# A list schedule for GateLoop and a SwiGLU feed-forward block: new transfer times and a new table of stage dates

## The chip, the cores and the metric

The kernel runs on one core of a Trainium2 chip. The time is that of one execution on the device, in microseconds (us). TensorE is called PE here, VectorE DVE, ScalarE ACT, GpSimd POOL, and SyncE SP; PEld are the weight loads of PE. SP issues most of the transfers, ACT and POOL a few.

## The reference

Inputs are q, k, v and complex gates a_re, a_im of shape (batch 4, heads 8, sequence 768, head size 48), and three weights: 384 x 1536 twice (gate and value) and 1536 x 384 (out), with a scale of 384.

```python
scale = np.minimum(mag, 0.999) / (mag + 1e-06)       # mag = |a|
for t in range(S):
    new_re = ar * S_re - ai * S_im                   # ar, ai: the scaled gate
    new_im = ar * S_im + ai * S_re
    S_re, S_im = (new_re + kv, new_im)               # kv = outer(k[t], v[t])
    y[:, :, t] = np.einsum('bhd,bhde->bhe', q[:, :, t], S_re)
# y, heads joined, is x: 3072 tokens x 384
xn = x / np.sqrt(np.mean(x * x, axis=-1, keepdims=True) + 1e-06) * rms_g
g = xn @ w_gate
silu = g * (1.0 / (1.0 + np.exp(-g)))
out = silu * (xn @ w_val) @ w_out
```

## The kernel before

**Work.** The sequence is cut into 24 chunks of 128 tokens, six to a batch. The recurrence within a chunk is a causal attention: running products of the gates, as magnitude and angle, are multiplied into q and k, and then scores, a mask and a product with v give the chunk's output; a state of 96 x 384 carries the rest from chunk to chunk. The gates are worked out in 13 units: chunk 0, chunk 1, then pairs (2, 3), (4, 5) and so on. The feed-forward part works on groups of chunks: [0], [1], [2, 3], [4, 5], [6, 7], [8, 9], [10 to 13], [14 to 17], [18 to 21], [22, 23]. From the group [4, 5] on, the gate and value products share a bilinear scheme of 15 products in place of 18 (`joint`), and the out product one of 7 in place of 8 (`down`, per pair of chunks).

**Stages of a chunk**, by the names that the tables use. `load` brings a unit's a_re and a_im into `in`, `kq` its q and k into `kin`. `size`, `root`, `turn` work out magnitude and angle on ACT and DVE (squares, scans along the tokens, arctan, sines). `rot` multiplies them into q and k, in `rot` and `kin`, and then six transfers on SP (three from `rot` and three from `kin`; six from `rot` for the first four chunks) lay the result into `kq`, features on partitions. From chunk 4 on there is one `kq` buffer, written anew for each chunk when the last reader is done. `decay` sends the unit's end values the same way, in six small transfers. `attend` is the scores on PE (`bank<-kq`) and the masked copy into `am` on DVE; `y` the product with v (`am,ve`) and the old state (`kq,state`); `state` the transposed k and its product with v (`vn,kt`). `norm` squares the output on ACT, sums it on PE (`ones,sq`), takes the power -1/2 on POOL, spreads the result over partitions by two transfers on POOL's queue (`sq<-rs`, `row<-sq`, chunks 4 to 21) and multiplies it into `xT` on DVE. `head` and `feed` are the gate and value products (`xT,wg`, `xT,wv`, and sums of both), the silu on ACT and the product into `hT`. `down` and `plain` are the out product (`wo,hT`, `sums,extra`, `wo,extra`), and its result goes through `ot` to the output.

**Weights.** They come as twelve pieces of wide words on POOL's queue, two ahead (`raw`), and are narrowed on ACT and DVE (`w`). The same pieces are later looked at again for the range check (`look`), by transfers on SP. At the end a sum over all checks, `okc`, goes through PE into a flag `bad`, which every engine reads; if it is set, a second, general path computes the output. That path did not run here.

**What sets the order.** Nothing is issued while the program is written. Each instruction is recorded by `add` with a modelled duration, and reads and writes give its dependencies. `dates` works out a due date for each from its users' due dates, backwards, and then adds a shift for its stage from a table of numbers (`flow.shift`). `schedule` plays the engines through: whenever an engine is free, it takes the ready instruction with the least due date. The result is the order on each engine, which `issue` then emits; on the chip each engine keeps that order and waits where an operand is late. So a modelled duration or landing decides only where something stands, and so do the shifts.

A transfer's modelled landing is its issue, plus a lead, plus its load (served one after the other for all queues) and 0.05, plus a number `slow` of its own, plus `LAND`:

```python
served = t + o["load"] + 0.05
o["landed"] = served + o["slow"] + self.LAND
```

An instruction on PE that uses another tile shape than the one before it is charged `between`; an operand that comes from PE to another engine is charged `delay`. Matmuls put in as fillers (`bank<-rot`) keep PE busy at the start, where the plan shows idle time there.

Of the kernel before, what the change touches and what calls it, by code (L numbers as in the profile page):

```python
# [19 lines left out]
P = 128  # L20
C = 128
# [480 lines left out]
class Flow:  # L502
# [8 lines left out]
    LAND = 1.0  # L511
    LANES = 8
    turn = 0.0
# [238 lines left out]
def fast(tc, ctx, qT, kT, v, a_re, a_im, w_gate, w_val, w_out, rms_g, out, H, bad):  # L752
# [4 lines left out]
    D2 = 2 * D  # L757
# [3 lines left out]
    ND = DM // P  # L761
# [252 lines left out]
    def fetch(i, piece, raw, eng):  # L1014
# [12 lines left out]
        pace = dict(load=1.9 + 1.0e-3 * raw.shape[1], lead=1.2) if eng == "POOL" else dict(slow=2.5)  # L1027
# [63 lines left out]
    def way_of(u):  # L1091
        return u if u < 2 else 2 + u % 2

    def load_gates(u):
# [28 lines left out]
    def load_kq(u, t):  # L1123
        flow.stage = "kq", u
        for name, ap in (("q", qT), ("k", kT)):
            for i, n in enumerate(UNITS[u]):
                dma(t[name][:, i],
                    ap[n].rearrange("d (h t) -> (d h) t", t=C).rearrange("(j p) t -> p j t", p=P),
                    slow=0.5 if u < 2 else 1.5, behind=moved[HOLD] if u > 1 else rows_, group=("kq", u))
        return t  # L1130

    def send_decays(u):
# [8 lines left out]
        for r in range(2 * ND):  # L1141
            dma(decays[way_of(u)][r:D2:2 * ND], ends[:, r % ND, ns[0]:ns[0] + len(ns)], behind=moved[max(ns[0], 1)])

    def gates(u):
# [65 lines left out]
        for i, n_ in enumerate(ns):  # L1210
# [4 lines left out]
            moved[n_] = [dma(kq[r:D2:2 * ND], x, "ACT" if n_ == 0 and r % 3 == 1 else "SP", slow=0.3) for r, x in enumerate(rows[n_])]  # L1215
# [23 lines left out]
    def attend(n):  # L1239
# [5 lines left out]
        later = dict(slow=1.5 if n > 1 else 0.4, behind=moved[min(n - 1, HOLD)] if n else (), group=("v", n))  # L1245
# [408 lines left out]
    for in_, limit, op in ((ef, P_MIN, ALU.is_ge), (ef, 1.0, ALU.is_le), (range_, 0.0, ALU.is_le),  # L1654
# [18 lines left out]
        ("attend", 0): -0.4, ("attend", 1): 9.6, ("attend", 2): -2.2, ("attend", 3): 7.4, ("attend", 4): 3.7,  # L1673
        ("attend", 5): -1.7, ("attend", 6): -0.2, ("attend", 7): -14, ("attend", 8): -2.2, ("attend", 9): -29.7,
        ("attend", 10): 1.8, ("attend", 11): -12.9, ("attend", 12): 23.5, ("attend", 13): -60, ("attend", 14): -24.3,
        ("attend", 15): -3.8, ("attend", 16): 6, ("attend", 17): -17.1, ("attend", 18): -10.1, ("attend", 19): -60,
        ("attend", 20): 17.6, ("attend", 21): -21.5, ("attend", 22): -15.4, ("attend", 23): -2.6, ("decay", 0): 1.5,
        ("decay", 1): -51, ("decay", 2): 22.6, ("decay", 3): -5, ("decay", 4): 35.9, ("decay", 5): 23.8,
        ("decay", 8): -26.5, ("decay", 9): -42.7, ("decay", 10): -7.4, ("decay", 11): -18.1, ("decay", 12): -14.3,
        ("down", 2): -60, ("down", 3): 27.5, ("down", 4): -3.1, ("down", 5): -0.5, ("down", 6): -32.8,  # L1680
        ("down", 7): 28.2, ("down", 8): -14.9, ("down", 9): 3.3, ("down", 10): 51, ("down", 11): -59.8,
        ("feed", 0): -5.6, ("feed", 1): -20.6, ("feed", 2): 17.7, ("feed", 3): 28.3, ("feed", 4): -18.2,
        ("feed", 5): 38.7, ("feed", 6): -8.4, ("feed", 7): 1.5, ("feed", 8): 0.3, ("feed", 9): -58.6,
        ("form", 0): 25.6, ("form", 1): -51, ("form", 2): 22.5, ("form", 3): -23.1, ("form", 5): -14,
        ("form", 7): 0.2, ("form", 8): -22.7, ("form", 10): 37.8, ("form", 11): -35.1, ("form", 13): 0.1,
# [3 lines left out]
        ("load", 3): 41.2, ("load", 4): -54.9, ("load", 5): -56.6, ("load", 6): 15.5, ("load", 7): -19.3,  # L1689
        ("load", 9): -33.2, ("load", 10): -25.3, ("load", 11): 34.6, ("load", 12): 30.5, ("look", 0): 58.9,  # L1690
        ("look", 1): 59.9, ("look", 2): 39.6, ("look", 3): 60, ("look", 4): 11.5, ("look", 5): -5.7,
        ("look", 6): -11.9, ("look", 8): -15.6, ("look", 9): -20.2, ("look", 10): -5.3, ("look", 11): 28.5,
        ("look", 12): -2.4, ("look", 13): 44.6, ("look", 14): -44.4, ("look", 15): -11.1, ("look", 16): 0.4,
        ("look", 17): 14, ("norm", 0): -2.6, ("norm", 2): 0.9, ("norm", 3): -18, ("norm", 4): 5.5, ("norm", 5): 3.5,
        ("norm", 6): -39.9, ("norm", 7): 46.3, ("norm", 8): -27.6, ("norm", 9): -1.2, ("norm", 10): -23.2,
        ("norm", 11): 60, ("norm", 12): -10.1, ("norm", 13): 0.5, ("norm", 14): -60, ("norm", 15): -16.2,
        ("norm", 16): 2, ("norm", 17): -27.7, ("norm", 18): -1.2, ("norm", 19): -37.3, ("norm", 20): -14,
        ("norm", 21): 3.6, ("norm", 22): 1.2, ("norm", 23): 3, ("plain", 1): -60, ("plain", 2): 26.3,
        ("raw", 0): -14.5, ("raw", 1): 48.4, ("raw", 2): 21, ("raw", 3): -2.5, ("raw", 5): -42.4, ("raw", 8): 15.2,
        ("raw", 9): 5.1, ("raw", 10): 0.6, ("raw", 11): 8.1, ("root", 0): 15.9, ("root", 1): -18.4,  # L1700
        ("root", 2): -43.8, ("root", 3): -27.2, ("root", 4): 5.3, ("root", 5): 0.2, ("root", 6): 39.8,
        ("root", 8): -21.9, ("root", 9): 8.8, ("root", 10): 1.6, ("root", 11): 47.9, ("root", 12): -12.7,
        ("rot", 0): 15.4, ("rot", 1): -6.2, ("rot", 2): 2.4, ("rot", 3): -15.8, ("rot", 4): 6.4, ("rot", 5): 58.6,
        ("rot", 6): -8.4, ("rot", 7): 55.6, ("rot", 8): -11, ("rot", 9): -8.4, ("rot", 10): 49.7, ("rot", 11): -7.2,
        ("rot", 12): 47.6, ("scale", 0): 56.3, ("size", 0): 1.9, ("size", 1): 1.2, ("size", 2): 22.4,
        ("size", 3): 60, ("size", 4): -17.9, ("size", 5): 40.8, ("size", 6): 1.5, ("size", 7): 2.1,
        ("size", 8): 43.3, ("size", 9): 12.6, ("size", 11): 15, ("size", 12): 32.8, ("state", 0): -47.3,
        ("state", 1): -29.6, ("state", 3): 10.3, ("state", 4): 1.8, ("state", 6): 30.7, ("state", 8): -2.7,
# [70 lines left out]
```

## Time and profile before

| | |
|---|---|
| median of three runs | 690.55 us (688.13 to 692.86) |
| the profiled execution | 689.29 us |
| its span, first to last instruction | 687.5 us |
| mean granted clock of PE | 0.995 |

The profiled execution has 1.8 us outside its span and stands 1.3 us under the median. All instructions of the plan carry one line, L749, at which `issue` calls them, so the views are read by tile names: `bank<-wo,hT` is a matmul with result in a PSUM bank and the operands `wo` and `hT` (buffer numbers left out). A release behind an arrow, as in `<-DVE hT`, names what ended the wait, by the event that came last. [...] In the table of transfers, KB are of one transfer, and the time is from its issue to its landing.

### The profile page before, as it was taken

The numbers are of one execution on the slowest core, as the hardware profiler recorded it, in microseconds if no ns is written. First come the engines' busy times: TensorE is split into PE (matmuls) and PEld (weight loads), VectorE is DVE, ScalarE is ACT, GpSimd is POOL, SyncE is SP. The second block draws the span as 40 slices with busy tenths as digits, with TensorE's granted clock in tenths as the row PEclk, the third lists the DMA queues.
The fourth block names the chain that finished last, engine by engine and source line by source line (L and its number), as shares of the span: only waits on it lengthen the run. The fifth ranks groups of instructions, "written<-read, shape, count | busy, mean of one in ns | idle before, by whom it ended". The sixth has DMA issues, their size and how long they took to land.

```text
span 687.5 us, 17763 instructions
## 1 busy us (share of the span) xinstructions
PE 643.0 (94%) x7272; PEld 575.6 (84%) x7274; DVE 551.6 (80%) x988; ACT 499.9 (73%) x861; POOL 61.0 (9%) x109
## 2 busy tenths in 40 slices
PE   0788989899999999999999999999999999999996
PEld 0778867786998999999978889978889888899995
DVE  8898998689998799978977899788989674574472
ACT  8988975896685767576679875388764258897792
POOL 3122200001100001100100001100003100000000
PEclk9999999999999999999999999999999999999999
DMA  9897543445425236574252264552244322547321
GB/s 284 285 286 205 182 128 92 104 88 122 126 29 120 68 81 138 109 145 81 35 127 71 40 132 98 109 139 31 55 98 95 76 81 81 197 141 242 125 74 45
DMA packets 104150, 81.90 MB, mean 119 GB/s; under 512 B 41952, under 2 KB 94560, under 8 KB 104064
## 3 DMA queue, kind: packets, MB, share of 16 engines
q1 hardware_dynamic: 98272, 64.42, 36.0%
q0 software_dynamic: 4416, 15.35, 10.4%
q8 instruction: 58, 0.95, 0.6%
q10 hardware_dynamic: 1376, 0.95, 0.5%
q14 instruction: 28, 0.23, 0.1%
HBM read 55.84 MB, written 4.72 MB: 88 GB/s over the span
## 4 chain that ended last, share of the span: by engine, by line
PE 37%; issue 28%; DMA 14%; DVE 11%; ACT 5%; POOL 2%; SPq 1%; ACTq 0%; POOLq 0%; DVEq 0%
PE bank L749 37%; DMA sq<-rs 6%; DMA row<-sq 3%; DVE rot L749 3%; DMA hT<-in_w_val_dram 2%; DVE in L749 2%; DMA wo<-in_w_val_dram 2%; POOL rs L749 1%; DVE extra L749 1%; ACT t L749 1%; SPq L749 1%; DVE wo L749 1%; DMA hT<-in_w_out_dram 1%; DVE t L749 1%; ACT rot L749 1%
## 5 line engine op out<-in xcount | busy, mean ns | idle before, releaser
L749 PE MATMUL bank<-wo,hT 128*128 128x192 f32 (+1 forms) x432 | 89.6, 358 | 1.7 <-DVE hT L749 1.7
L749 PE MATMUL bank<-xT,wg 128*128 128x128 f32 (+1 forms) x416 | 80.8, 322 | 3.4 <-ACT sg L749 1.6
L749 ACT ACTIVATE extra<-bank 128x512 f32<-128x512 f32 x100 | 58.1, 595 | 35.3 <-PE bank L749 27.1
L749 PEld LDWEIGHTS bank<-wo,hT 128*128 128x128 f32 x432 | 71.4, 190 | 12.8 <-DVE hT L749 1.9
L749 PE MATMUL bank<-xT,wv 128*128 128x128 f32 (+1 forms) x416 | 79.7, 319 | 0.0
L749 PEld LDWEIGHTS bank<-xT,wg 128*128 128x128 f32 x416 | 61.5, 191 | 9.4 <-ACT sg L749 1.8
L749 PEld LDWEIGHTS bank<-xT,wv 128*128 128x128 f32 x416 | 63.0, 193 | 5.0
L749 ACT ACT_TABLE_LOAD x47 | 60.3, 1283 | 3.1 <-issue 2.3
L749 POOL TENSOR_TENSOR rs<-ssv,mhalf 128x1 f32<-128x1 f32 x24 | 21.9, 913 | 449.6 <-ACT ssv L749 386.5
L749 ACT ACTIVATE bank<-bank 128x512 f32<-128x512 f32 x60 | 35.0, 584 | 22.4 <-PE bank L749 11.6
L749 ACT ACTIVATE sg<-bank 128x512 f32<-128x512 f32 (+1 forms) x71 | 37.9, 536 | 12.3 <-PE bank L749 7.8
L749 DVE TENSOR_TENSOR in<-in,t 128x1536 f32<-128x1536 f32 (+1 forms) x26 | 42.3, 1627 | 4.3 <-ACT in L749 4.0
L749 PE MATMUL bank<-wo,extra 128*128 128x192 f32 x240 | 45.2, 329 | 0.3 <-DVE extra L749 0.3
L749 DVE COPY_PREDICATED am<-causal,bank 128x512 f32<-128x512 int32 x48 | 34.8, 731 | 12.5 <-PE bank L749 12.3
L749 DVE TENSOR_TENSOR extra<-bank,extra 128x512 f32<-128x512 f32 x50 | 34.3, 687 | 12.8 <-ACT bank L749 4.7
L749 PEld LDWEIGHTS bank<-kq 96*32 96x32 f32 x1536 | 30.5, 110 | 16.4 <-issue 6.8
L749 PE MATMUL bank<-kq 96*32 96x128 f32 (+3 forms) x1536 | 36.3, 237 | 6.1 <-DMA kq<-rot 2.1
L749 ACT ACTIVATE in<-in 128x768 f32<-128x768 f32 (+1 forms) x45 | 36.1, 805 | 6.2 <-DVE in L749 5.9
L749 PEld LDWEIGHTS bank<-wo,extra 128*128 128x128 f32 x240 | 39.6, 190 | 1.1 <-DVE extra L749 0.6
L749 PE MATMUL bank<-am,ve 128*32 128x128 f32 x768 | 37.8, 275 | 0.1
L749 PE MATMUL bank<-kq,state 96*32 96x128 f32 x640 | 32.4, 272 | 0.0
L749 DVE TENSOR_TENSOR bank<-bank,extra 128x512 f32<-128x512 f32 x30 | 20.8, 695 | 14.1 <-ACT extra L749 10.5
(247 smaller groups left out, 1565.7 us busy)
## 6 DMA issues: line engine op xcount, KB each, us to landing
kq<-rot SPq DMA_DIRECT2D x82, 128.0 KB, 2.5
kq<-kin SPq DMA_DIRECT2D x60, 128.0 KB, 2.5
kin<-in_q_dram SPq DMA_DIRECT2D x24, 192.0 KB, 4.1
kin<-in_k_dram SPq DMA_DIRECT2D x24, 192.0 KB, 3.8
in<-in_a_re_dram SPq DMA_DIRECT2D x11, 384.0 KB, 5.0
in<-in_a_im_dram SPq DMA_DIRECT2D x11, 384.0 KB, 5.4
out_dram<-ot SPq DMA_DIRECT2D x22, 192.0 KB, 2.1
vn<-in_v_dram SPq DMA_DIRECT2D x20, 192.0 KB, 4.0
```

The costliest lines, as they stand in the source:

```text
L749: fn(*args, **kw)
```

## The change

No instruction of the computation is added or removed. Three kinds of numbers change, and with them the order of nearly everything.

First, the planner's times: the landing that is common to all transfers (`LAND`), the delay from PE to the other engines, the price of another tile shape, and the `slow` or `load` of each kind of transfer. Second, all numbers of `flow.shift`, of which the diff below shows a line. Third, by consequence, two fillers fewer (30 for 32) and one load of an ACT function table more (48 for 47). The groups stay as they are.

```diff
-    LAND = 1.0
+    LAND = 0.7
...
         if o["eng"] == "PE":
-            return 0.2
+            return 0.25
...
         if o["mode"] is not None:
-            return 0.225 if o["stage"][0] == "attend" else 0.09
+            return 0.13 if o["stage"][0] == "attend" else 0.09
...
-        pace = dict(load=1.9 + 1.0e-3 * raw.shape[1], lead=1.2) if eng == "POOL" else dict(slow=2.5)
+        pace = dict(load=1.9 + 1.0e-3 * raw.shape[1], slow=0.3, lead=1.2) if eng == "POOL" else dict(slow=0.5)
...
             x = dma(t[name], ap[b].rearrange("(h j l) s -> l h j s", j=ND, l=L)[:, :, :, c * C:c * C + T],
-                    "ACT" if u < 2 and name == "im" else "SP", slow=0.75 if u < 2 else 2.5, behind=moved[HOLD] if u > 1 else (),
+                    "ACT" if u < 2 and name == "im" else "SP", slow=1.05 if u < 2 else 0.5, load=None if u < 2 else 1.9, behind=moved[HOLD] if u > 1 else (),
                     due=u - 310.0 if u < 2 else None)
...
-                    slow=0.5 if u < 2 else 1.5, behind=moved[HOLD] if u > 1 else rows_, group=("kq", u))
+                    slow=0.8 if u < 2 else 1.0, behind=moved[HOLD] if u > 1 else rows_, group=("kq", u))
...
-            dma(decays[way_of(u)][r:D2:2 * ND], ends[:, r % ND, ns[0]:ns[0] + len(ns)], behind=moved[max(ns[0], 1)])
+            dma(decays[way_of(u)][r:D2:2 * ND], ends[:, r % ND, ns[0]:ns[0] + len(ns)], load=0.15, slow=0.3, behind=moved[max(ns[0], 1)])
...
-            moved[n_] = [dma(kq[r:D2:2 * ND], x, "ACT" if n_ == 0 and r % 3 == 1 else "SP", slow=0.3) for r, x in enumerate(rows[n_])]
+            moved[n_] = [dma(kq[r:D2:2 * ND], x, "ACT" if n_ == 0 and r % 3 == 1 else "SP", slow=0.9 if n_ < 2 else 0.15) for r, x in enumerate(rows[n_])]
...
-        later = dict(slow=1.5 if n > 1 else 0.4, behind=moved[min(n - 1, HOLD)] if n else (), group=("v", n))
+        later = dict(slow=0.8 if n > 1 else 0.7, behind=moved[min(n - 1, HOLD)] if n else (), group=("v", n))
...
-            dma(line, rss[n % 2], "POOL", lead=1.2)
+            dma(line, rss[n % 2], "POOL", slow=1.2, lead=1.2)
             wide = row
-            dma(wide, line.unsqueeze(1).to_broadcast([1, P, C]), "POOL", load=2.0, lead=1.2)
+            dma(wide, line.unsqueeze(1).to_broadcast([1, P, C]), "POOL", load=2.0, slow=0.3, lead=1.2)
...
-        ("attend", 0): -0.4, ("attend", 1): 9.6, ("attend", 2): -2.2, ("attend", 3): 7.4, ("attend", 4): 3.7,
+        ("attend", 0): -46.6, ("attend", 1): 8.4, ("attend", 2): -33.3, ("attend", 3): 4.1, ("attend", 4): -39.8,
```

What this does to the order shows at three places. The first is SP's queue at chunk 4: the six transfers into `kq0`, the gates `in0` of chunks 6 and 7, and the decays of chunks 4 and 5. Before:

```order
L749 DMA kq0_111<-rot0_109 16x8x256 x2
L749 DMA in0_103<-in_a_re_dram 128x3x256
L749 DMA kq0_111<-rot0_109 16x8x256
L749 DMA kq0_111<-kin_105 16x8x256
L749 DMA in0_103<-in_a_im_dram 128x3x256
L749 DMA kq0_111<-kin_105 16x8x256 x2
L749 DMA decay3_116<-ends_88 16x8x2 x6
```

And now:

```order
L749 DMA kq0_111<-rot0_109 16x8x256 x3
L749 DMA kq0_111<-kin_105 16x8x256 x3
L749 DMA in0_103<-in_a_re_dram 128x3x256
L749 DMA in0_103<-in_a_im_dram 128x3x256
L749 DMA decay3_116<-ends_88 16x8x2 x6
```

The two loads moved from between the six transfers to behind them. At chunk 14 the load of re stays among them and that of im goes; at chunks 13 and 18 one load or none is left, and at chunk 6 both loads have moved in.

The second place is PE at the end of the gate and value products of chunks 4 and 5 and the start of their out product; `xT2,in1` and `xT2,kq1` are the last of the products, and `wo,hT` into bank 1 needs what becomes of them. Before:

```order
L749 MATMUL bank3_72<-wo_98,hT_99 128x192 x3
L749 MATMUL bank1_70<-xT2_102,in1_104 128x128 x2
L749 MATMUL bank1_70<-xT2_102,kq1_112 128x128 x2
L749 MATMUL bank1_70<-wo_98,hT_99 128x192 x6
L749 MATMUL bank3_72<-wo_98,hT_99 128x192 x3
```

And now:

```order
L749 MATMUL bank0_69<-wo_98,hT_99 128x192 x3
L749 MATMUL bank1_70<-xT2_102,in1_104 128x128 x2
L749 MATMUL bank1_70<-xT2_102,kq1_112 128x128 x2
L749 MATMUL bank0_69<-wo_98,hT_99 128x192 x3
L749 MATMUL bank7_76<-ones_80,sq0_128 128x1
L749 MATMUL bank5_74<-vn0_125,kt0_121 32x48 x24
L749 MATMUL bank1_70<-wo_98,hT_99 128x192 x6
L749 MATMUL bank3_72<-wo_98,hT_99 128x192 x6
```

Three products of the out product, a sum of squares and the state's product of chunk 6 moved in between.

The third is the end of PE's work. Before:

```order
L749 MATMUL bank0_69<-wo_98,extra_108 128x192 x3
L749 MATMUL bank3_72<-wo_98,extra_108 128x192 x3
L749 MATMUL bank0_69<-sums_138,hT_99 128x192 x6
L749 MATMUL bank3_72<-wo_98,extra_108 128x192 x3
L749 MATMUL bank7_76<-ones_80,okc_143 1x1
```

And now:

```order
L749 MATMUL bank0_69<-wo_98,extra_108 128x192 x3
L749 MATMUL bank7_76<-ones_80,okc_143 1x1
L749 MATMUL bank3_72<-wo_98,extra_108 128x192 x3
L749 MATMUL bank0_69<-sums_138,hT_99 128x192 x6
L749 MATMUL bank3_72<-wo_98,extra_108 128x192 x3
```

The sum over the checks moved ahead of the last twelve products, and DVE's instruction that makes `bad` of it with it. Elsewhere, of the same kinds: ahead of the first products on `xT` of the groups [14 to 17] and [18 to 21], more other PE work stands behind the last sum of squares; on ACT the first narrowing copy of a weight piece to fp16 stands ahead of the sines of chunk 0, which it followed.

More of the change, by code (lines that the diff above doesn't have):

```diff
@@ L1672, in fast @@
     flow.shift = {
-        ("attend", 0): -0.4, ("attend", 1): 9.6, ("attend", 2): -2.2, ("attend", 3): 7.4, ("attend", 4): 3.7,
[L1674 to L1682, printed above, removed]
@@ L1691, in fast @@
[L1691 to L1700, printed above, removed]
@@ L1701, in fast @@
[L1701 to L1705, printed above, removed]
@@ new lines, in fast @@
+        ("decay", 12): 22.7, ("down", 2): -5.3, ("down", 3): 28.5, ("down", 4): -4.5, ("down", 5): 52.8,
+        ("down", 7): 29.8, ("down", 8): -5, ("down", 9): 2.6, ("down", 10): 7.6, ("down", 11): -60,
+        ("feed", 0): 16.8, ("feed", 1): 5.9, ("feed", 2): 29, ("feed", 3): -4.3, ("feed", 4): -9.6,
+        ("feed", 5): 15.7, ("feed", 6): -3.8, ("feed", 7): 1.4, ("feed", 8): -59.3, ("feed", 9): -56.7,
+        ("form", 0): -17.1, ("form", 1): 22.1, ("form", 2): -13.4, ("form", 3): -7.8, ("form", 4): -60,
@@ new lines, in fast @@
+        ("form", 5): -3.4, ("form", 6): -52.5, ("form", 7): 4.2, ("form", 8): 14.5, ("form", 9): 10.9,
+        ("form", 10): 14, ("form", 11): 3.3, ("form", 12): 8.4, ("form", 13): 1.5, ("head", 0): 3.8,
+        ("head", 1): -0.5, ("kq", 0): 1.8, ("kq", 1): -4.2, ("kq", 2): -59.5, ("kq", 3): 5.6, ("kq", 4): 10.5,
+        ("kq", 5): -32.2, ("kq", 7): 60, ("kq", 8): -14.6, ("kq", 9): -3.6, ("kq", 10): -49.1, ("kq", 11): 9.3,
+        ("kq", 12): -16.3, ("load", 0): -3.4, ("load", 1): 49.7, ("load", 2): 9.8, ("load", 3): 45.7,
@@ new lines, in fast @@
+        ("load", 5): -8, ("load", 6): 1.3, ("load", 7): 2.2, ("load", 8): 2.8, ("load", 9): -8.7, ("load", 10): 5.4,
+        ("load", 11): 59.1, ("load", 12): -48.2, ("look", 0): 5.9, ("look", 1): -38.3, ("look", 2): 3,
+        ("look", 3): -25, ("look", 4): 19.5, ("look", 6): 25.2, ("look", 7): 49.4, ("look", 8): 34.5,
+        ("look", 9): -33.9, ("look", 10): 1.4, ("look", 11): 56.6, ("look", 12): -60, ("look", 13): 1.9,
+        ("look", 14): 14, ("look", 15): 39.7, ("look", 16): 5, ("norm", 0): -2.2, ("norm", 1): -1, ("norm", 2): 8.1,
@@ new lines, in fast @@
+        ("norm", 3): -44.3, ("norm", 4): -60, ("norm", 5): 2.4, ("norm", 6): 28.6, ("norm", 7): 6,
+        ("norm", 8): -20.3, ("norm", 9): -6.7, ("norm", 12): -36, ("norm", 13): -3.5, ("norm", 15): 32.6,
+        ("norm", 16): 3.5, ("norm", 17): 0.1, ("norm", 18): 0.8, ("norm", 19): 3.2, ("norm", 20): -13.2,
+        ("norm", 21): -7, ("norm", 22): -51.7, ("norm", 23): 0.1, ("plain", 0): 1, ("plain", 1): -39.3,
+        ("plain", 2): 56.3, ("raw", 0): -0.4, ("raw", 1): 31.8, ("raw", 2): -1.1, ("raw", 3): 44.9, ("raw", 4): 33.3,
@@ new lines, in fast @@
+        ("raw", 5): -37.4, ("raw", 6): -38.8, ("raw", 7): -35.6, ("raw", 8): -13.2, ("raw", 9): 16.6, ("raw", 10): 2,
+        ("root", 0): -2.8, ("root", 1): -1.2, ("root", 2): -3.1, ("root", 3): 60, ("root", 4): -36,
+        ("root", 5): 20.9, ("root", 6): 46.8, ("root", 7): 1.7, ("root", 8): -41.8, ("root", 9): -7.4,
+        ("root", 10): -0.5, ("root", 11): 9.3, ("root", 12): 4.2, ("rot", 0): -51.8, ("rot", 1): -10.7,
+        ("rot", 2): -16, ("rot", 3): -1.2, ("rot", 4): -1.3, ("rot", 5): 6.3, ("rot", 6): 5.7, ("rot", 7): 59.8,
@@ new lines, in fast @@
+        ("rot", 8): -3.3, ("rot", 9): 36.5, ("rot", 10): -3.9, ("rot", 11): -9, ("rot", 12): -43.9,
+        ("scale", 0): 27.9, ("size", 0): -8.4, ("size", 1): -27.8, ("size", 2): 7.9, ("size", 3): 9.4,
+        ("size", 4): -53.9, ("size", 5): 12.3, ("size", 6): 10.2, ("size", 7): 15.4, ("size", 8): 45.4,
+        ("size", 9): 20.1, ("size", 10): 2.2, ("size", 11): 0.6, ("size", 12): 38.2, ("state", 0): 10.8,
+        ("state", 1): 4, ("state", 2): 48.7, ("state", 3): -0.4, ("state", 4): -12.8, ("state", 6): 57.4,
```

24 lines of the change are left out of this document (11 added, 13 removed), and 15 rows, old and new, of the table filler.

## Prediction

> **What bounds the kernel now.** I read the page's totals first, then TensorE's (PE's) waits in two windows, then the granted clock where it isn't 1, then the lines around each wait. The totals: columns are busy time, share of the span, instructions.
>
> ```profile
> span 687.5 us, 17763 instructions
> PE 643.0 (94%) x7272; PEld 575.6 (84%) x7274; DVE 551.6 (80%) x988; ACT 499.9 (73%) x861; POOL 61.0 (9%) x109
> ```
>
> PE is busy for 643.0 of 687.5 us. The change gives PE the same matmuls but for two fillers, so it can win only out of the 44.5 us in which PE idles, or out of a slow clock. The waits of PE up to 80 us (in total, times, longest), where the weights arrive:
>
> ```profile
> PE bank L749 <- DVE ot L749: 17.6, 2, 15.7
> PE bank L749 <- DVE rot L749: 2.5, 1, 2.5
> PE bank L749 <- DMA kq<-rot: 1.8, 1, 1.8
> PE bank L749 <- ACT sg L749: 1.6, 1, 1.6
> PE bank L749 <- issue: 1.4, 1, 1.4
> ```
>
> And from 80 us on:
>
> ```profile
> PE bank L749 <- DVE am L749: 2.3, 2, 1.2
> PE bank L749 <- DVE xT L749: 2.0, 2, 1.1
> PE bank L749 <- DMA kq<-kin: 2.0, 3, 1.5
> PE bank L749 <- DVE hT L749: 1.8, 2, 1.7
> PE bank L749 <- DMA decay<-ends: 1.8, 1, 1.8
> PE bank L749 <- DVE extra L749: 0.8, 2, 0.5
> ```
>
> The front holds some 25 us of idle PE, the long middle 12, the end after PE's last product 6.4 (687.5 less 680.86 + 0.19, the end of the last matmul, below). The middle's waits are single late operands, none of them a lasting shortage: this is what an order of work can mend. One of them has a second cost. The table of windows gives stretch, busy time of PE, PEld, DVE, ACT, POOL (with counts), the granted clock, DMA share and GB/s:
>
> ```profile
> 126.00:128.00 2.00, 1.08 (x56) 1.11 (x60) 0.22 (x1) 1.97 (x4) 0.00 (x0) 0.93 0.16 16
> 128.00:130.00 2.00, 2.00 (x28) 1.82 (x20) 1.81 (x3) 2.00 (x4) 0.00 (x0) 0.50 0.62 180
> 130.00:132.00 2.00, 2.00 (x8) 1.69 (x8) 2.00 (x3) 2.00 (x4) 0.00 (x0) 0.72 0.05 11
> ```
>
> Shortfalls of 0.07, 0.50 and 0.28 times 2.00 us make 1.7 us of PE work lost just behind the 1.8 us wait.
>
> **Transfers of k and q.** From chunk 4 on one buffer `kq` holds the operands of the scores, filled by six transfers on SP. The plan before put loads of the next gates between them:
>
> ```profile
> 116.70 1.23 SPq L749 DMA_DIRECT2D kq<-rot  x2
> 118.03 0.61 SPq L749 DMA_DIRECT2D in<-in_a_re_dram  x1
> 118.69 0.63 SPq L749 DMA_DIRECT2D kq<-rot  x1
> 119.42 0.55 SPq L749 DMA_DIRECT2D kq<-kin  x1
> 120.07 0.61 SPq L749 DMA_DIRECT2D in<-in_a_im_dram  x1
> 120.74 1.26 SPq L749 DMA_DIRECT2D kq<-kin  x2
> 126.92 0.55 PE L749 MATMUL bank<-kq 96*32 96x128 f32 x17 [1.82 <-DMA decay<-ends]
> ```
>
> The releaser is put down to the last event, `decay<-ends`. I read it as kq: the scores take no decays, the scores' operands are the transfers queued behind both loads, and the transfers' medians from 100 to 680 us (KB each, us to landing) say what stands in their way:
>
> ```profile
> kq<-rot SPq DMA_DIRECT2D x60, 128.0 KB, 2.5
> in<-in_a_re_dram SPq DMA_DIRECT2D x9, 384.0 KB, 5.0
> in<-in_a_im_dram SPq DMA_DIRECT2D x9, 384.0 KB, 5.3
> ```
>
> The last kq issue begins near 121.4 and PE starts at 126.92, 5.5 us later, where 2.5 is the median. A load of 5.0 or 5.3 us in front makes that difference. After the change both loads stand behind all six (first piece of the order above): the last issue is 2 x 0.65 us earlier, and its landing some 3 us shorter. That is more than the 1.8 wanted, so this wait goes: -1.8. In the same way chunk 14 keeps re between its transfers and loses im (the longest of the three kq<-kin waits, 1.5; half of what stood in front is gone, taken -1.4), and chunks 13 and 18 lose theirs (the other 0.5 of that row). Together -3.7. What hides those loads afterwards is the time to their own unit's gates, which begin a chunk later. The reverse edit is at chunk 6: it gets re and im between its six transfers, where none stood; nothing in the trace shows it, so bound: 0 (the landing stood 4.4 us ahead of the scores), and 1.8, the wait that chunk 4 has now. It goes into the new waits below.
>
> **The groups of four.** Two waits for xT, 0.9 and 1.1 us, stand ahead of the gate-and-value products of chunks 14 to 17 and 18 to 21: norm by GpSimd, two transfers and one multiplication must pass after the last sum of squares. Counting matmuls in the order by their spacing, PE work between that sum and the first product on xT grows from 10.2 to 12.1 us and from 9.6 to 11.2, by 1.9 and 1.6: both waits are covered: -2.0. If the cover fails, they return whole.
>
> **The product down of chunks 4 and 5.** The wait of 1.7 for hT:
>
> ```profile
> 213.69 3.19 PE L749 MATMUL bank<-wo,hT 128*128 128x192 f32 x18 [1.67 <-DVE hT L749]
> 216.72 1.14 PE L749 MATMUL bank<-sums,extra 128*128 128x192 f32 x6
> 217.70 0.49 PE L749 MATMUL bank<-wo,extra 128*128 128x192 f32 x2
> ```
>
> The group of the state's update (busy us, mean ns):
>
> ```profile
> L749 PE MATMUL bank<-vn,kt 128*32 128x48 f32 x960 | 17.9, 207 | 0.0
> ```
>
> Six such records, which are three lines of the order, take 217.70 - 216.72 = 0.98 us, 0.163 each. Before, nothing lies between the product pair `xT,in`, `xT,kq` and the down product that needs its result. After (second piece of the order) three such lines (0.98) and the state's update lie between; the update takes 17.9 us over 20 chunks (the last of a batch has none), 0.90. The sum, 1.9, covers 1.67; taken -1.5, since VectorE's order there changes too. In the last down product, the wait for `extra` (the longest of its two, 0.5) gets 2.9 us more cover, 18 records at 0.163: -0.5. Of the two waits for am, chunk 3's second scores move ahead by about a third of a us: -0.3. These and the two parts before make **-8.0** in the middle.
>
> **The clock.** The slow stretch is the only one between 10 and 680 us and follows the wait at chunk 4 at once. If it is due to the wait, it goes with it: -1.7; if not, 0. I take **-1.7**, since no other, shorter wait is followed by one. The Trainium skill, "TensorE: Matmul & The Clock Gate", Part 1: The HAM clock gate, has the half clock come after at least one idle window of about 3.4 us and calls the window free-running. The trace differs in the first: half clock came here with 1.82 us of unbroken idle time. By that rule the wait would not be its cause and the term would be 0.
>
> **The end.** PE's last work, the check's sum over `okc`, the flag `bad` made of it, and the last store:
>
> ```profile
> 680.86 0.19 PE L749 MATMUL bank<-ones,okc 128*1 128x1 f32 x2
> 681.24 0.14 DVE L749 TENSOR_SCALAR bad<-bank 1x1 int32<-1x1 f32 x1
> 681.35 0.36 SPq L749 DMA_DIRECT2D out_dram<-ot  x1
> L1735 POOLq TENSOR_LOAD <-bad x1: 589/589/589, 681.4 to 681.4; - x1
> 682.00:687.50 5.50, 0.00 (x0) 0.00 (x0) 0.00 (x0) 0.00 (x0) 0.00 (x0) 0.69 0.09 27
> ```
>
> Every engine loads `bad`, branches and closes. In the records behind these views, GpSimd's closing drain runs from 682.65 to 686.64 and all others have finished by 684.27; the last barrier takes 0.8. After the change the sum over `okc` and `bad` stand ahead of the last 12 products (third piece): 12 x 2 records at 0.163 = 3.9 us. GpSimd has nothing else to do there, so its load and drain run beside products, and SP's closing sets the end: 686.64 - 684.27 = **-2.4**; bounds 0 (the drain waits for the others) and -2.4 (SP's path is untouched).
>
> **The front.** ScalarE's first narrowing copy of a weight piece to fp16 moves ahead of chunk 0's sines, and the kq transfers of chunks 0 and 1 go later; a copy and a transfer beside the weights take:
>
> ```profile
> L749 ACT ACTIVATE wo<-wo 128x1536 f16<-128x1536 f32 x2 | 7.3, 3659 | 0.0
> kq<-rot SPq DMA_DIRECT2D x6, 128.0 KB, 8.9
> 60.00:100.00 40.00, 36.97 (x460) 31.73 (x460) 38.70 (x57) 34.56 (x46) 6.36 (x12) 1.00 0.57 164
> ```
>
> From 60 to 100 us VectorE is busy 38.70 of 40.00: what the front loses counts only if it delays VectorE's work on chunks 2 and 3, whose operations are the same set before and after. Bounds: -1.6 (the wait for sg goes) and +3.7 (the copy passes through whole). Taken **+0.5**, near the hidden end because of that row. **Mode.** Two more segments of PE work with other tile shapes: two of 82, at most a quarter us each by the planner's constants: **+0.5**. Two fillers and one table load more: hidden, the first in idle time of the front, the second on ScalarE (73% busy).
>
> **New waits.** The new order has its own thin places: chunk 6, the score buffers of chunks 9 to 21 (5.5 to 7 us of PE work ahead of a chain of about 5), the covers above. Nothing shows their price. Below: 0; above: 8.0, as much as goes. I take **+3.5**, somewhat under the middle, because the planned landings are now near the recorded ones for the transfers that made the waits.
>
> **Sum:** -8.0 - 1.7 - 2.4 + 0.5 + 0.5 + 3.5 = -7.6. The profiled execution took 689.29 (span 687.5), so 681.7; the median of the runs, 690.55, stands 1.26 above it: **683.0**.
>
> **Rivals.**
> (a) Waits form anew: VectorE (80%) and the kq chain get as late elsewhere as they were; new waits 8.0 and another slow stretch 1.7. For it: every one of the middle's waits was planned away once by the same program. Against: landings are now closer. -2.4 + 1.0 = -1.4: 689.2. Chance 0.17.
> (b) The drain stays last: it is held by a barrier. Against it: it starts 0.2 us before SP's first closing step. 685.4; 0.10.
> (c) The front passes through: +3.7 in place of +0.5: 686.2; 0.06.
> (d) The other side, slower. Re and im are now planned to land after 1.2 + 1.9 + 0.05 + 0.5 + 0.7 = 4.35 us (the planner's constants), against 5.0 and 5.3 recorded (in the plan before: 5.9). If gates start on them that late at 11 units and PE waits for each, the other terms (-2.4 - 4.3 + 1.0 = -5.7) are used up from 0.52 us per unit on; at 1.2 us it is 689.29 - 5.7 + 13.2 + 1.26 = 698.1. Against it: the middle's waits above name no wait of PE that goes back to a late load. 0.06.
> (e) The clock's rule: the slow stretch comes from the activity around scores and not from the wait, so it stays: 683.0 + 1.7 = 684.7; 0.09. This is the rule of the page cited above; the trace disagrees on the idle time.
>
> **How the numbers follow.** My forecast has the remaining 0.52. Its own range is 677.5 (no new waits, -3.5; the front -2) to 687.5 (half of the middle's gain missing). With (a), (b), (c), (e) inside, the range is 677.5 to 690.5; outside are (d) and the ends, under 0.2. About 1% is what a measurement of this kernel can tell from no change: below 683.6 counts as faster, above 697.5 as slower. Of my forecast's 0.52 some 0.33 lie below 683.6, of (b), (c) and (e) 0.07: faster 0.40. Slower is most of (d): 0.05. The rest 0.55.
>
> **What would show it.** Chunk 4's scores start without a wait and no window there shows a clock under 0.9; no PE wait for xT from 80 us on; none for hT near 212; the flag `bad` about 4 us before PE's last product and some 4 us between that product and the span's end in place of 6.4. The prediction is wrong if PE's waits from 80 us on sum to over 8, if chunk 1's scores start over 2 us later, or if new waits name in<-in_a_re or in<-in_a_im.

## The result, and the profile after

The changed kernel takes 686.0 us (median of 20 runs, 680.53 to 692.74), the kernel before 690.48 (20 runs, 686.83 to 692.86). The ratio is 0.9935, with a 95% interval of 0.9912 to 0.9957 (it compares runs within 1.5% of each kernel's fastest; the spread itself is explained below). The forecast was 683.0, within 677.5 to 690.5. The change is some 4.5 us faster, where 7.5 were expected.

The totals of the changed kernel's profile, whose execution took 684.15 us:

```profile
span 682.4 us, 17723 instructions
PE 642.8 (94%) x7270; PEld 577.1 (85%) x7270; DVE 549.0 (80%) x988; ACT 498.6 (73%) x862; POOL 72.0 (11%) x109
```

A matmul of the program stands in the trace as two records (the 30 fillers are 60). PE's busy time is the same as before (643.0), so the 5.1 us that the span lost are nearly all idle time: counted from the records, PE's last matmul ends 2.8 us earlier (678.27 for 681.05), and from there to the end it takes 4.16 in place of 6.42. PE's waits up to 80 us, and then from 80 us on (in total, times, longest; three more rows of 0.2 and 0.3 us are left out):

```profile
PE bank L749 <- DVE ot L749: 15.8, 1, 15.8
PE bank L749 <- DVE rot L749: 7.5, 1, 7.5
PE bank L749 <- ACT sq L749: 2.5, 1, 2.5
```

```profile
PE bank L749 <- DMA kq<-kin: 3.9, 3, 1.5
PE bank L749 <- DMA kq<-rot: 1.4, 1, 1.4
PE bank L749 <- DVE am L749: 1.2, 1, 1.2
PE bank L749 <- ACT bank L749: 0.6, 1, 0.6
PE bank L749 <- ACT rot L749: 0.6, 1, 0.6
PE bank L749 <- ACT extra L749: 0.5, 1, 0.5
PE bank L749 <- DMA decay<-ends: 0.4, 1, 0.4
```

The rows for xT (2.0) and hT (1.8) are gone, and so is the wait of 1.8 ahead of chunk 4. In their place stands kq, at other chunks: by the records 1.38 us at chunk 2, 1.35 at chunk 12, 1.04 at 14, 0.38 at 16 and 1.51 at 17. Counting those that are left out, the rows fell only from 11.9 to 9.3 in sum. The end of the flag, by the tile `bad`:

```profile
L749 DVE TENSOR_SCALAR bad<-bank x1: 140/140/140, 674.2 to 674.2; 1x1 int32<-1x1 f32 x1
L1736 POOLq TENSOR_LOAD <-bad x1: 498/498/498, 674.4 to 674.4; - x1
```

The flag is there 4 us before PE's last product, and GpSimd reads it at once. And the table of windows (stretch, busy PE, PEld, DVE, ACT, POOL, the granted clock, DMA share, GB/s) shows what was not expected:

```profile
52.00:54.00 2.00, 0.41 (x4) 0.23 (x4) 1.41 (x3) 1.12 (x1) 1.02 (x2) 1.00 1.15 228
54.00:56.00 2.00, 1.07 (x9) 1.07 (x10) 1.86 (x2) 2.00 (x7) 0.56 (x1) 1.00 0.92 145
56.00:58.00 2.00, 2.00 (x12) 2.00 (x12) 1.53 (x1) 2.00 (x5) 1.73 (x2) 0.52 1.02 342
58.00:60.00 2.00, 2.00 (x13) 1.98 (x12) 0.00 (x0) 1.97 (x3) 0.67 (x1) 0.62 0.68 130
...
93.00:95.00 2.00, 0.62 (x27) 0.49 (x30) 1.86 (x3) 1.79 (x2) 0.00 (x0) 1.00 0.73 198
95.00:97.00 2.00, 1.35 (x55) 1.07 (x44) 2.00 (x3) 1.74 (x3) 0.00 (x0) 1.00 0.60 164
97.00:99.00 2.00, 1.44 (x16) 1.18 (x20) 2.00 (x4) 0.92 (x3) 0.00 (x0) 0.51 0.54 131
99.00:101.00 2.00, 2.00 (x48) 1.85 (x44) 2.00 (x7) 0.00 (x0) 0.00 (x0) 0.50 0.15 10
101.00:103.00 2.00, 2.00 (x58) 1.94 (x53) 0.33 (x2) 0.90 (x4) 0.00 (x0) 0.50 0.15 32
103.00:105.00 2.00, 2.00 (x61) 1.94 (x55) 1.49 (x3) 1.10 (x4) 0.00 (x0) 0.78 0.84 237
```

The half clock at 128 us is gone, but behind the wait for ACT at 52 us and behind the two waits of chunk 2 (for kq, then for am) stand new stretches at half clock: 3.4 us and 6.8 us, three times what there was.

### The profile page after: what moved, and what is told of

Its sections match the earlier page's. It is cut to its first block, busy times and chain, and to the rows that moved or that the text cites. A ratio compares the mean times of both kernels' runs of the same rounds, so it can differ in the third digit from the quotient of the medians.

```text
span 682.4 us, 17723 instructions
## 1 busy us (share of the span) xinstructions
PE 642.8 (94%) x7270; PEld 577.1 (85%) x7270; DVE 549.0 (80%) x988; ACT 498.6 (73%) x862; POOL 72.0 (11%) x109
## 5 line engine op out<-in xcount | busy, mean ns | idle before, releaser
L749 POOL TENSOR_TENSOR rs<-ssv,mhalf 128x1 f32<-128x1 f32 x24 | 28.4, 1185 | 454.3 <-ACT ssv L749 427.3
L749 ACT ACTIVATE sg<-bank 128x512 f32<-128x512 f32 x71 | 37.5, 532 | 7.5 <-PE bank L749 4.9
```

Source lines behind the costliest of these rows:

```text
L749: fn(*args, **kw)
```

## The experiments

The theory to begin with: the waits are made by where an instruction stands, so they recur and can be moved, and the half clock follows them. Its rivals say that the clock falls at random, that SP's slow issues are an accident, that what is saved in one place is waited for at the next, or that nothing but the pair of numbers and table counts.

In the small diffs below, `behind` and `warm` are helpers of a few lines: `behind(chunks)` puts the loads that stand among a chunk's six kq transfers just behind them on SP, and `warm(stage, i, bank, n)` puts n matmuls of the identity into a free bank ahead of the stage's i-th instruction on PE. `flags` are the sum over `okc` and the flag `bad`, `spot` PE's other instructions in their order. A difference with ± below is one between means, with its 95% interval, from the scatter of the runs that the ratios use; "at equal clock" means that one common slope of time against mean granted clock was taken out first.

**1. The changed kernel again**, with no edit.

> The changed kernel itself, unaltered, as the measure for the three runs beside it and to see which of its waits recur. Theory W (the waits are fixed by the order): median 686 (683 to 689), PE again waits 1.0 to 1.6 us for kq at chunks 2, 12 and 17 and for am at chunk 2, and none for xT. Rival S (the waits of chunks 12 and 17, where one issue on SP took 2.64 and 2.24 us instead of 0.6, are an accident of that execution): those two are under 0.3 this time, and the run's span is some 2 to 3 us shorter at the same clock. Theory K (the half clock follows stretches with little PE work): the profile shows half clock only between 50 and 110 us and in the tail. Rival R (it falls at random): half clock at other places too, behind full stretches.

Measured: 686.63 us (12 runs, ratio 0.9939 to the kernel before, 0.9901 to 0.9976). Its profile:

```profile
PE bank L749 <- DMA kq<-kin: 3.4, 3, 1.6
PE bank L749 <- ACT sq L749: 3.3, 1, 3.3
...
PE bank L749 <- DMA kq<-rot: 1.3, 1, 1.3
PE bank L749 <- DVE am L749: 1.3, 1, 1.3
```

The waits recur at the same chunks (1.65 at 12, 1.46 at 17, 1.3 at chunk 2 for kq and again for am), so they belong to the order. That at chunk 14 stayed away this time, and one for ACT at 551 us grew to 1.7. The clock falls to a half at the same places too, 56.8 and 97.8 us. Chance is in how many of these windows an execution gets: over the 20 runs of the change, time and mean clock go together with a correlation of -0.86, from 680.53 us at a clock of 1.000 to 689.64 and more at 0.985. A line through them falls by 6.9 us for each 0.01 and stands at 680.7 at full clock; the kernel before, in the 33 runs beside this and the next three, has -0.74 and 684.9.

**2. The flag late.**

```diff
+    for i, x in enumerate(flags):
+        x["order"] = spot[-1]["order"] + 900.0 + i
```

> The changed kernel with the sum over okc and the flag bad put back behind the last product. Theory T (GpSimd's closing drain, about 4 us from the flag on, sets the end): from PE's last product to the end of the span 6.4 us in place of 4.1, the time 2.3 us over the unaltered changed kernel. Rival (the end is set by the last store's path anyway): within 0.5 us of it.

Measured: 688.39 us (12 runs), 1.8 over the unaltered kernel beside it; ratio to the kernel before 0.9966 (0.9932 to 0.9999). The end of its profile, span 681.7:

```profile
675.08 0.19 PE L749 MATMUL bank<-ones,okc 128*1 128x1 f32 x2
...
675.46 0.14 DVE L749 TENSOR_SCALAR bad<-bank 1x1 int32<-1x1 f32 x1
675.57 0.33 SPq L749 DMA_DIRECT2D out_dram<-ot  x1
```

From PE's last matmul (675.08 + 0.19) to the end it is 6.4 us again, for 4.2 with the early flag. By the records GpSimd's closing drain takes 3.99 us in both profiles. Here it ends at 680.87, 2.4 us behind SP's own last closing step (678.50), so it sets the end; in the profile of the change it ends at 679.56 and SP's step, at 681.51, comes last. In the profiles the tail is worth 2.3, about what was forecast. The times alone do not settle it: the difference to run 1 is 1.6 us (±2.9), at equal clock 0.8 (±1.5). This execution also shows what the clock does: its wait for `sq` at 53 us was 0.84 us in place of 3.3 in run 1, it had one half-clock window in the middle and not three, and its span is 3.8 us shorter than that of run 1, although it has the longer end.

**3. All loads behind the kq transfers.**

```diff
+    behind(range(4, N))
```

> The changed kernel with every load that stands on SP between the six kq transfers of a chunk (from chunk 4 on) put behind the six. Theory Q (a load in front makes the transfer land late): PE's waits for kq at chunks 12, 14, 16 and 17, 4.3 us in the profile of the change, go to under 1 in sum, and the time falls by 2.5 to 4 us. Rival G (the loads are wanted: put back, they make the gates of the next unit or v late): the kq waits go, but waits for gates' work or for v come, and the time is within 1 us or higher. Rival S (the late landings come from SP's own slow issue): the waits at 12 and 17 stay.

Measured: 688.22 us (12 runs), 1.6 over run 1, which is not certain (2.2 ±2.4 by the means; the mean clock is 0.9903 for 0.9929); ratio 0.9956 (0.9925 to 0.9987). PE's waits from 200 to 400 us:

```profile
PE bank L749 <- ACT extra L749: 2.3, 1, 2.3
PE bank L749 <- ACT kt L749: 1.6, 1, 1.6
PE bank L749 <- issue: 0.3, 1, 0.3
```

The waits for kq are gone, and waits for ACT have come. Just ahead of the first of them ACT stands in its own order behind an instruction whose gates are not there:

```profile
352.76 0.41 ACT L749 ACTIVATE mid<-sg 128x256 f32<-128x256 f32 x1
355.91 0.93 ACT L749 ACTIVATE t<-in,mid 128x768 f32<-128x768 f32 x1 [2.75 <-DMA in<-in_a_re_dram]
356.75 0.58 ACT L749 ACTIVATE extra<-bank 128x512 f32<-128x512 f32 x1
```

PE needed `extra`, third in this list, and it waits because the load of a_re, moved back by three microseconds, holds up the instruction ahead of it. So a load between the kq transfers costs the scores, and behind them at chunks 8 and 14 costs ACT; with the second of these waits come 6.8 us at half clock, from 356.9 us on. It was rival G, but not at every chunk: at 12, 16 and 17 nothing new came.

**4. Fillers against the half clock.**

```diff
+    warm(("norm", 1), 0, 5, 10)
+    warm(("attend", 2), 0, 6, 6)
+    warm(("state", 2), 1, 6, 5)
```

> The changed kernel with 21 filler matmuls (10, 6 and 5, each about 0.22 us at full clock) ahead of the three instructions that wait longest between 50 and 100 us. Theory K (half clock follows a stretch with little PE work): the half clock between 55 and 105 us is gone or halved, mean clock up by 0.003 to 0.006, the time 1.5 to 4 us under the unaltered changed kernel. Rival R (the clock's falls have nothing to do with these waits): mean clock as before, the time the same or up to 1 us longer. Rival D (from 50 to 100 us the bound is VectorE, so a faster PE only waits longer): the clock rises and the time stays within 1 us.

Measured: 683.31 us (10 runs, 681.64 to 686.15), 3.3 under run 1 (1.8 ±2.3 by the means); ratio 0.9903 (0.9876 to 0.9931). The profile's line of the core:

```profile
core 0: 682.8 us, clock 1.000
```

Mean clock over the runs is 0.9985, for 0.9929 in run 1 and 0.9938 for the kernel before, and the spread shrank from 10.8 to 4.5 us. So the half clock does follow the waits: matmuls that compute nothing, put into them, keep the clock. They are not free: run 1's fit to full clock is 680.2, 3 us less than this kernel shows. In its profile the scores of chunk 4 start 2.1 us later than in run 2 (127.52 for 125.42), and those of the chunks behind it 2.5 to 3.5 later; how much of it the fillers make, and how much VectorE's load there, was not separated.

**5. The kernel before, with chunk 4's loads behind its transfers.**

```diff
+    behind([4])
```

> The kernel before with one edit: at chunk 4 the loads of re and im stand behind the six kq transfers instead of between them. Theory Q with K (the load in front makes the wait, and the wait makes the half clock): the wait of 1.8 us at chunk 4 is gone, the window after it is at full clock, and the time falls by 1.8 to 3.5 us. Rival R (the half clock there is no consequence of the wait): the wait goes, the half clock stays near 128 us, -1.8 or less. Rival G (the loads are then late for chunks 6 and 7): the wait goes and another of over 1 us comes ahead of chunk 6; the time within 1 us.

Measured: 688.48 us (12 runs) beside 690.13 of the kernel before; ratio 0.9981 (0.9947 to 1.0016), so not certain in time. In the profile it is plain; these windows held a wait and a half clock before:

```profile
126.00:128.00 2.00, 2.00 (x73) 1.90 (x62) 1.37 (x2) 1.83 (x3) 0.00 (x0) 1.00 0.35 39
128.00:130.00 2.00, 2.00 (x10) 1.76 (x10) 0.01 (x1) 1.98 (x3) 0.00 (x0) 1.00 0.27 80
130.00:132.00 2.00, 2.00 (x56) 1.65 (x58) 0.33 (x1) 1.99 (x4) 0.00 (x0) 1.00 0.39 117
```

The wait and the half clock at 128 us are gone together, with one edit on SP. In this execution another window fell to half, at 303 us, behind a wait of 1.4; the span did not change by the 3.5 us that both were worth (687.6 for 687.5). PE's waits from 80 us on are 12.0 in sum, for 11.9 before: others came, as 1.02 for `sq` at 157 us, and that at 302 grew from 0.65 to 1.38. The mean clock of its runs is 0.9959, for 0.9941 of the kernel before, and at equal clock the difference in time is +0.5 us (±1.3). So the edit moved the wait and the half clock with it, but that the removed wait shortens the run by its 1.8 us is not shown; part of it at least was waited for further on.

**6. The kernel before, with the flag two microseconds earlier.** Here the checks are ready later than in the changed kernel, so it is six matmul lines before the end and not twelve.

```diff
+    for i, x in enumerate(flags):
+        x["order"] = max(spot[-3]["order"], flow.ops[-3]["order"]) + 0.1 + 0.1 * i
```

`flow.ops[-3]` is DVE's instruction that makes `okc`.

> The kernel before with one edit: the sum over okc and the flag bad stand ahead of the last six matmuls of the order, 2 us earlier, which is as early as the checks are ready there. Theory T: from PE's last product to the end of the span 4.1 to 4.4 us in place of 6.4, the time 2 to 2.3 us under the kernel before. Rival (nothing else of the end is ready): within 0.5 us.

Measured: 688.82 us beside 690.13; the ratio is 1.0009 (0.998 to 1.0037), so the times show no gain: 2 us less would be 0.997, outside the interval, and at equal clock the difference is +0.5 us (±1.3). In the profile the flag stands at 678.9 and PE's last matmul ends at 681.0, and the span is 685.4: 4.4 us in place of 6.4, as expected. The end of the profile is as theory T says; why the runs as a whole are not faster stays open (in the profile PE's waits from 80 us on sum to 12.9, for 11.9 before).

```profile
L749 DVE TENSOR_SCALAR bad<-bank x1: 147/147/147, 678.9 to 678.9; 1x1 int32<-1x1 f32 x1
L1740 POOLq TENSOR_LOAD <-bad x1: 503/503/503, 679.1 to 679.1; - x1
```

**7 and 8. One part of the change alone.** Number 7 has the new planner's numbers with the old table, number 8 the old numbers with the new table; the diffs are the two halves of the change.

> The new transfer times and other planner numbers with the old table of stage dates. Theory P (the dates are fitted to the numbers, each table is only good with its own): slower than the kernel before, 692 to 705. Rival N (nearer numbers alone give a better order): faster, 684 to 689, and then the new table adds little.

> The old planner numbers with the new table. Theory P: slower than the kernel before, 692 to 705, as the dates were found against other landings. Rival M (the table is what matters): 684 to 689, as the whole change.

Measured: 749.38 us (4 runs, ratio 1.0872, 1.0821 to 1.0922) and 732.27 (4 runs, 1.0634, 1.0577 to 1.069). The direction is that of theory P, the size is far beyond what it expected. PE's longest rows from 80 us on, of 7 and then of 8:

```profile
PE bank L749 <- DMA kq<-kin: 10.9, 3, 8.1
PE bank L749 <- ACT extra L749: 6.3, 8, 2.5
PE bank L749 <- ACT kt L749: 4.2, 2, 3.1
```

```profile
PE bank L749 <- DMA kq<-kin: 9.7, 3, 4.3
PE bank L749 <- DVE wo L749: 5.0, 1, 5.0
PE bank L749 <- DVE sq L749: 4.8, 2, 3.5
```

In sum the rows from 80 us on are 40.0 and 41.2, for 11.9 before. The mean clock is 0.9615 and 0.9678, for 0.9941; at the slopes of run 1 that is, as an estimate, 22 to 28 of the 59 us lost in number 7 and 18 to 23 of the 42 in number 8. The likely reason, argued and not followed through the plan: a due date moves an instruction only against what else is ready at that moment; other landings make other things ready, and a table found for the one plan puts wrong ones in front in the other. The change is one piece: 59 us worse with the first half, 42 with the second, 4.5 better with both.

**9. Only the loads that may move.**

```diff
+    behind([12, 16, 17])
```

> The changed kernel with the loads behind the six kq transfers at chunks 12, 16 and 17 alone, where moving them brought no new wait in the run that moved all. Theory Q (a load in front makes the landing late): the waits for kq at these three chunks (1.35, 0.4 and 1.5 us in the profile of the change) go to under 0.5 in sum, and the time at equal clock falls by 2 to 3 us; median 682.5 to 684.5. Rival S (SP's own slow issue makes them): 17 or 12 still waits over 1 us. Rival A (what is saved is waited for further on): waits go, time within 1 us of 686.

Measured: 683.69 us (6 runs), ratio 0.9903 (0.9872 to 0.9935). PE's waits from 280 to 440 us in the changed kernel, and then here:

```profile
PE bank L749 <- DMA kq<-kin: 3.9, 3, 1.5
PE bank L749 <- DMA decay<-ends: 0.4, 1, 0.4
```

```profile
PE bank L749 <- DMA kq<-kin: 1.5, 1, 1.5
PE bank L749 <- issue: 0.6, 1, 0.6
```

What is left of kq is chunk 14, which was not moved. The rows fall by 2.2 us, and the fit to full clock, of six runs, stands at 677.6, for 680.2 to 680.7 without the edit. Against the 20 runs of the changed kernel the means differ by 2.2 us (±2.4), at equal clock by 2.2 (±1.5). So the loads moved at three chunks are worth about half of what the whole change brought, with a wide margin. At chunks 12 and 16 the waits stay away in the profiles of the next three runs too, which have the same edit; at chunk 17 they do not (below).

**10, 11 and 12. Both, and a mask ahead of a multiplication.** Number 10 adds fewer fillers than run 4 had (5, 4, 4). Number 11 adds to it that VectorE takes chunk 2's masked copies first:

```diff
+    wide_["order"] = am_[1]["order"] + 0.01
```

`wide_` is the multiplication `in<-in,t` of 1.75 us, `am_` the two masked copies.

Number 12 is number 11 with ten fillers in place of five at the first place.

> The same with fillers as well, 5, 4 and 4 in place of the 10, 6 and 5 that held the clock. Theory K (a window of 3.4 us with PE busy for about half or less is followed by half clock; 1 us more of work in it is enough): no half clock between 50 and 110 us, mean clock 0.996 or more, and fewer fillers cost less: median 679.5 to 682. Rival (5, 4 and 4 are too few): half clock as without, median 682 to 685. Rival D (VectorE bounds this stretch): clock full, time 682 to 684.

> The same, and VectorE takes the two masked copies of chunk 2 ahead of the 1.75 us multiplication of the gates that stands in front of them. Theory V (that multiplication makes the 1.2 us wait for am): the wait for am at chunk 2 is under 0.4, the time 0.5 to 1.2 us under the run without this edit. Rival D (VectorE is busy through, so the multiplication's own users now wait as long): the wait goes, another of about a microsecond comes between 97 and 130 us, time the same within 0.5.

> The run before with 10 fillers instead of 5 ahead of the sum of squares of chunk 1, where 5 left a wait of 2.6 us and a half-clock window in one profile. Theory K: no window between 50 and 110 us is below 0.6 busy, mean clock over 0.997 in nearly every run, median 680 to 682 with a narrower spread than without (under 6 us). Rival D (the front is bound by the weights' arrival, and fillers that end after the sum's operands delay it): clock as good, but median 682 to 684, no better than with 5.

Measured: 683.25 us (ratio 0.988, 0.9851 to 0.9909), 681.68 (0.986, 0.9829 to 0.9891) and 681.87 (0.9869, 0.9826 to 0.9912), 6 runs each. In number 10's profile the two places at chunk 2 kept the clock, while at the first one five fillers were too few: the sum's operands were late by another 2.56 us, and half clock followed; another step at half clock, at 354.7 us, followed a wait of 2.31 for kq at chunk 14. In number 11 the wait for am is gone (1.2 us without fillers, 0.3 with those of number 10), and PE's waits between 90 and 135 us are:

```profile
PE bank L749 <- DMA kq<-rot: 1.4, 2, 1.0
PE bank L749 <- DVE state L749: 1.4, 1, 1.4
```

The waits that rival D announced came, 1.4 for the state and 1.0 for the next kq, but not for its reason: VectorE is not full there. Ahead of the `state` that PE waits for, it stands idle itself, in number 11 and in number 12:

```profile
103.00 0.56 DVE L749 TENSOR_TENSOR state<-state,decay 96x384 f32<-96x384 f32 x1 [2.14 <-issue]
102.95 0.56 DVE L749 TENSOR_TENSOR state<-state,decay 96x384 f32<-96x384 f32 x1 [1.76 <-DMA decay<-ends]
```

In number 11 SP issues the twelve kq transfers of chunks 2 and 3 and the six decays nearly without a pause from 86.5 to 99.6 us, and by the records the last decay lands at 102.73. What comes next to hold up PE here is thus the transfers and not VectorE. The waits for kq further on also changed: at chunk 10 PE waits 1.64, 1.87 and 0.64 us in the three profiles (0.47 in run 4, under 0.3 without fillers), and at chunk 17 0.92, 1.31 and 1.27, though no load stands among its transfers.

Number 12 holds the clock better (mean 0.998, with one step at half clock in its profile, at 103.7 us; 680.4 to 684.69, a spread of 4.3 us) and is no faster by its median than number 11, whose runs go from 677.79 to 692.47. By their medians numbers 11 and 12 beat the kernel before by 1.3 to 1.4% and the change by some 4 us.

## Why the prediction was right, and where not, point by point

All five signs that it named for itself came (chunk 4, xT, hT, the flag, the end). Of the three that it named against itself, two came as well: PE's waits from 80 us on sum to 9.3, over 8 (10.7 in run 1), and chunk 1's scores start over 2 us later. No wait of the change names the loads of the gates. So the way and the range held, while the terms for new waits and for the clock did not.

**Right: the tail.** -2.4 was forecast and 2.3 came, in the profile of the change and, by putting the flag back, in that of run 2. In the times, runs 2 and 6 do not show it beyond noise. Rival (b) fell: in the profile of the change the drain ends 1.95 us ahead of SP's last step (679.56 and 681.51).

**Right: the waits that it named.** xT -2.0, hT at 212 us, chunk 4's kq -1.8 and the wait ahead of the last `sums,extra` are gone; those for am fell by 1.1, more than the 0.3 taken. Chunk 14 was mis-sized: re stayed among its transfers, and of 1.5 us it still waits 1.04, where -1.4 was taken. That the wait is gone does not mean that its 1.8 us are won (run 5). That the row with `decay<-ends` was really kq is borne out by the landings and by run 5. Before, the last kq transfer landed at 126.78 us, 0.14 ahead of the scores. In run 5, which moves nothing but the two loads, it landed at 123.35 and the scores start at 125.77, ahead of the decays, which stayed behind the loads and land up to 129.26.

**Right while the clock holds: the front.** Chunk 1's scores start 2.4 us later (45.83 for 43.44). Yet in run 2, which has that order and no half clock there, chunk 1 starts 3.2 later than before and chunk 2 0.15 earlier, which fits the argument that VectorE's full stretch hides it. Where half clock follows the wait for `sq` at 52 us, chunk 2 starts later too, by 2.4 us in the change and 3.4 in run 1 (94.54 and 95.53 for 92.13); the term of +0.5 did not have that.

**Mis-sized: new waits.** +3.5 was taken, out of 0 to 8.0. From 80 us on the rows went from 11.9 to 9.3; some 8.9 of the old went, so new ones of 6.3 came. The thin places that the forecast listed were not the ones: chunk 6 waits 0 with both loads among its transfers, and chunks 12, 16 and 17, with one load each, wait 3.2 together. At 12 and 17, SP itself took 2.64 and 2.24 us for one issue in the profile, against about 0.6 (below). With the loads out of the way (run 9) both waits went; that of chunk 12 stayed away in all five profiles with its load moved, so there the load is the cause, while that of chunk 17 came back in runs 10 to 12.

**Failed: the clock.** The step said: the slow stretch follows the wait at chunk 4, so it goes with it, -1.7. The first half is true (run 5), and rival (e), by which it would stay, fell. The step left out that the new waits would make their own. Behind 52 us and behind 93 us three steps of 3.4 us are at half clock where there was one, and over the runs the mean clock did not rise but fell, from 0.9938 (33 runs) to 0.9919 (20 runs; 0.9929 in the 12 of run 1). At the slope of 6.9 to 8.7 us for 0.01 that is +0.6 to +1.7 in place of -1.7. This error of 2.3 to 3.4 us and the 2.8 of new waits are more than the 3.0 between forecast and result; against them, the old waits fell by 0.9 more than forecast, and the half us for tile shapes did not show in PE's busy time. That leaves 0.7 to 1.8 us too much, which is not accounted for: the waits are those of one execution, the clock that of 20. The lines at full clock say it from another side: from 684.9 to 680.2 or 680.7, 4.2 to 4.7 us were won, where the forecast without its clock term had 5.9. That the result lies well inside the range is in part due to its width, 13 us, three times the effect.

The prediction also took the slow stretch at 128 us for the only one from 10 us on. The clock's first record in that profile is at 25.3 us, and the view shows 1.00 ahead of it; but the records of the fillers stand 0.213 us apart up to there and 0.112 behind it, so PE ran at half clock until then, before the change as after it (28.8 us). And a wait as long as that of chunk 4, 1.84 us ahead of chunk 1's scores, was not followed by half clock, so its length alone does not decide.

Rival (a), new waits as large as the old and another slow stretch, came nearest of the rivals in what happened: 6.3 of 8.9, and two steps more at half clock. By its number (c) stands nearest, 686.2, which is luck: a front that passes through whole is not what the runs show. Rival (d), late gates, does not show in the change, but run 3 shows its mechanism as soon as the loads move back: 2.75 us of ACT, 2.3 of PE.

## What to carry to other kernels

Where PE waits for one late operand, ask what the wait does to the clock as well: a wait of 2 us can cost another 1.7 behind it, and two short ones that fall close together twice that (1.38 and 1.21 at chunk 2, with 6.8 us at half clock behind them). A list schedule made from a table of dates leaves single misplaced instructions which the trace names and one line mends; look on the transfer queue first, check what the moved load holds up on the engine that needs it, and count the waits of the whole kernel again, since one that is gone can come back elsewhere (run 5). A table of dates and the times that it was found with are one thing: neither is of use alone.

## What the runs showed of the hardware

**Half clock after a half-busy window.** The granted clock changes on a grid of 3.41 us: in each of the twelve profiles used here all its changes lie a whole number of such steps apart. I cut twelve profiles (before, after, runs 1 to 6 and 9 to 12) from 30 to 678 us into these steps and added up PE's matmul records. Every step at full clock with PE busy for less than half of it was followed by half clock (7 of 7, busy shares 0.06 to 0.47). Between 0.52 and 0.65 it went both ways (nine to half, as 0.53 at 93.6 us after the change; others not, as 0.56 at 421 us). Above that one step alone, of 0.74 in run 12, was followed by half clock; it held, among others, scores and products with the state in tiles of 96 or 128 by 32, and whether these count for less was not tried. The Trainium skill, "TensorE: Matmul & The Clock Gate", Part 1: The HAM clock gate, names an idle window of about 3.4 us; the length and the free-running grid agree with these traces, but the window need not be idle: a half-idle one is enough. Three steps at half clock that were not full (0.74 to 0.85) were followed by another at half clock, and so was a full one in run 3, behind a step of 0.06. Before the change, the wait of 1.84 us ahead of chunk 1 touched steps that were still 0.69 busy or more, and full clock went on.

**The spread is the clock.** The runs of the two kernels vary by 6 to 12 us, and more than half of it goes with the mean granted clock (correlations of -0.74 to -0.88 in the sets above, which is 0.55 to 0.77 of the variance). Where the grid falls against the span's start differs from profile to profile, by anything from 1.3 to 3.4 us into a step, so a wait of 2 to 3 us may or may not fill half a step. Fillers in three waits took the spread from 10.8 to 4.5 us.

**SP's issues stretch.** An issue on SP takes about 0.6 us. Of 462 in the change's profile 28 took over 0.9, up to 2.64; by the records, 20 of these overlap a 16 KB packet of the instruction queue; of the 434 shorter ones 28 do. In the profile before it is 18 of 26, and 30 of 436. The two that hurt, at chunks 12 and 17, do not. They share something else: they begin 1.28 and 1.00 us after POOL issued `row<-sq`, the transfer that spreads a row over all partitions, and before it landed, some 4 us after its issue. In the twelve profiles, from 80 us on, 16 issues took over 1.9 us without such a packet, and all 16 began while a `row<-sq` was under way, 1.0 to 2.0 us after its issue; of all 4908 issues there it is 594. That the transfer is the cause is not shown, since no run moved it. It is not the load among the kq transfers: in run 3, with the load behind them, an issue of 3.08 us stands at chunk 12 all the same, and no wait over 0.3 us followed it. At chunk 17 the same transfer is the untested rival to the load: in runs 10 to 12 the last kq transfer, issued within 0.3 us of `row<-sq`, took 4.6 to 4.9 us to land, and in run 9, issued 0.4 us ahead of it, 2.4.
